# Attention feeding a two-expert mixture on one Trainium2 core: the front of the kernel reordered across GpSimd, VectorE, ScalarE and the queues

## The chip, the cores and the metric

The kernel runs on one core of a Trainium2 chip. A core has a matrix engine, TensorE (PE in the profile, with PEld for its weight loads), VectorE (DVE), ScalarE (ACT), GpSimd (POOL) and SyncE (SP), which here only issues transfers. Each engine works through its own list of instructions in order, and instructions of different engines meet at semaphores. 16 DMA engines move data between HBM and the on-chip memory.

The metric is the device time of one execution in microseconds. Three runs of the kernel before took 718.5, 725.89 and 728.75 us; their median, 725.89 us, is the number to compare with. One further execution was profiled.

## The reference

A causal linear attention with a decay per head is followed by a mixture of eight experts, of which each token uses two.

```python
def _attn_ref(q, k, v):                       # 4 batches, 8 heads, 768 tokens, 64 wide
    for t in range(S):
        state = gamma * state + outer(k[:, :, t], v[:, :, t])
        y[:, :, t] = scale * (q[:, :, t] @ state)

def _moe_ref(x, w_gate, w_noise, noise, w1, w2):   # x: 3072 tokens x 512
    noisy = x @ w_gate + log1p(exp(x @ w_noise)) * noise
    top2 = np.argpartition(-noisy, 2, axis=1)[:, :2]
    top2_w = softmax over the two
    for e in range(8):                         # w1[e]: 512 x 1024, w2[e]: 1024 x 512
        h = np.maximum(x[mask] @ w1[e], 0.0)
        out[mask] += top2_w * (h @ w2[e])
```

## The kernel before

The work has three stages on the same core.

**The chunk loop** (the loop over `j` in `range(NCH)`, 24 iterations) computes attention for 128 tokens at a time. Six chunks make a batch (`NC = 6`). Iteration `j` issues, in this order: the scores of the next chunk on PE (`qk(j+1)`, L311); on GpSimd the scaled values of the next chunk and the scaled queries of the one after (`v_scale`, tile `vp`, L285; `q_scale`, tile `qs`, L291); loads of chunk `j+4` on the SP queue; on VectorE the masked scores (`masked(j+1)`, tile `am`, L318) and the low half of the last output (`x_lo`, L352); the work listed in `between[j]`; then on PE the output of chunk `j` (`y_mm`, L325, L329, and the state update `pU`, L334) and the router's logits of chunk `j-3` (L364, L367); last the work listed in `todo[j]`. ScalarE copies the state (`U`, L340), sums squares (`junk`, L343) and writes the high half `x` (L348). The first chunk of a batch has no L329, the last no L334. The scores' PSUM has three buffers and a chunk uses two, so `qk(j+1)` waits for the first mask of chunk `j`.

**Routing.** For each batch `b`, steps `route_a` to `route_g` run on VectorE some iterations later, as `todo` places them. `route_e(b, k)` builds one-hot tables `ob` (L492) and `a` (L494) and multiplies three of five value planes into `bb` (L501); `route_e2(b, k)` does the other two planes on GpSimd (L501 too). `table(b)` is twelve matmuls over `a` and `bb` (L511), `route_f` adds their result to `acc`, `slots` turns it into row numbers `idx`, and `gather` fetches 128 rows of `xbuf` by an indirect transfer that GpSimd issues (tile `xg`, L621). `x_t` transposes them into `xe` through the SP queue. `places(b)` (L423) needs the choice of experts, `mb`, from `route_b2`.

**Expert weights.** A matrix comes in four parts. Each is loaded into `wst` (`w_load`, SP), its squares are summed on ScalarE (`w_sum`, L180), and then one scale for the four is made through a tiny matmul on PE (`w_scale`, L184). `w_hi` (L197, ScalarE) writes the high half. The low half comes in one of two ways:

```python
    def w_lo(e, which, i):
        nc.vector.scalar_tensor_tensor(lo, st[:, i * 1024:(i + 1) * 1024], sc[:, 0:1], hi,
                                       op0=OP.mult, op1=OP.subtract)

    def w_lo_pool(e, which, i):
        nc.scalar.activation(s, s, AF.Copy, scale=sc[:, 0:1])
        nc.gpsimd.tensor_tensor(lo, s, hi, op=OP.subtract)
```

The first is one VectorE instruction (L202); the second is one of ScalarE (L209) and one of GpSimd (L210).

**The early units.** After the loop, expert 0 starts on tokens that are already routed while the last batch is still being routed. Twenty `units` hold PE work: eight first products over 384 columns (`mm1`, L715 to L717, each followed by `hh` on ScalarE, L718, and `hl` on VectorE, L719), three second products (`mm2`, L745 to L747), eight first products over 192 columns, one more `mm2`. `early(n)` issues the next `n`; between the calls stand the routing steps. The first unit reads the 384 columns of `xe` that the first three gathers fill. `pH`, the PSUM of `mm1`, has three buffers, each freed by `hl`. `ranks()` orders the experts by load (L541 to L560, all on VectorE); the loads of the next expert need its result.

**The experts** then run one after the other, each with its next expert's weights prepared beside it.

Of the kernel before, what the change touches and what calls it, by code (L numbers as in the profile page):

```python
# [19 lines left out]
B, H, S, D = 4, 8, 768, 64  # L20
C = 128
NC = S // C
NCH = B * NC
# [11 lines left out]
B0 = B // 2  # L35
# [3 lines left out]
NBLK, CAP = 7, 832  # L39
CAPS = [832, 832, 816, 800, 800, 784, 768, 768]  # L40
NCOL = NBLK * E
# [53 lines left out]
def moe_kernel(ctx, tc, qT, kT, kt, vt, noise, wgn, w1, w2, ctab, qtab, xbuf, out):  # L95
# [434 lines left out]
    def rows_of(tk, n0, n1):  # L530

        padv = work.tile([128, NCOL], F32, name="padv")
        nc.vector.tensor_scalar(padv[:, n0:n1], tk[:, n0:n1], 0.0, K("pad"), op0=OP.is_equal, op1=OP.mult)
        nc.vector.scalar_tensor_tensor(idx[:, n0:n1], tk[:, n0:n1], 127.0, padv[:, n0:n1], op0=OP.add, op1=OP.add)

    def ranks():

        m = E - 1
        n, s3, s4 = R["cum"][:, 1:E], [128, m, m], [128, m, NBLK, m]
        key = hp.tile([128, m], F32, name="key")  # L540
        nc.vector.scalar_tensor_tensor(key, n, 8.0, K("tie"), op0=OP.mult, op1=OP.add)  # L541
        cm = hp.tile(s3, F32, name="cm")
        nc.vector.tensor_tensor(cm, key[:, None, :].to_broadcast(s3), key[:, :, None].to_broadcast(s3), op=OP.is_gt)
        rk = hp.tile([128, m], F32, name="rk")
        nc.vector.tensor_reduce(rk, cm, axis=AX.X, op=OP.add)
        pm = hp.tile(s3, F32, name="pm")
        nc.vector.tensor_tensor(pm, rk[:, None, :].to_broadcast(s3),
                                K("i64")[:, :m, None].to_broadcast(s3), op=OP.is_equal)
        nc.vector.tensor_tensor(cm, pm, K("lidx")[:, None, 1:E].to_broadcast(s3), op=OP.mult)
        nc.vector.tensor_reduce(rk, cm, axis=AX.X, op=OP.add)  # L550
        nc.vector.tensor_copy(eid, rk)
        tp = wp = hp.tile(s4, F32, name="tp")
        for t, a, d in ((tp, tk, tk), (wp, wacc, wacc)):
            v = a[:, NBLK:].rearrange("p (e t) -> p t e", e=m)
            nc.vector.tensor_tensor(t, v[:, None].to_broadcast(s4), pm[:, :, None, :].to_broadcast(s4), op=OP.mult)
            nc.vector.tensor_reduce(d[:, NBLK:].rearrange("p (r t) -> p r t", r=m), t, axis=AX.X, op=OP.add)
        rows_of(tk, NBLK, NCOL)
        nc.vector.tensor_tensor(cm, pm, K("rcap")[:, :, None].to_broadcast(s3), op=OP.mult)
        nc.vector.memset(capd, float(CAP))
        nc.vector.tensor_reduce(capd[:, 1:E], cm.rearrange("p r e -> p e r"), axis=AX.X, op=OP.add)  # L560
# [43 lines left out]
    def at(j, f, *a):  # L604
        todo.setdefault(j, []).append((f, a))
# [25 lines left out]
    between = {}  # L631
    for b in range(B - 1):
        n = (b + 1) * NC
        steps = [(2, route_a, b), (3, route_b, b), (4, route_b2, b), (4, route_c, b), (5, route_h, b), (5, route_d, b),
                 (6, route_e, b, 0), (6, route_e2, b, 0), (7, route_e, b, 1), (7, route_e2, b, 1), (8, route_f, b),
                 (8 if b == 0 else NCH - 1 - n, route_g, b)]
        if b == B - 2:
            steps = [(2, route_a, b), (3, route_b, b), (3, route_b2, b), (4, route_c, b), (4, route_h, b), (5, route_d, b)]
        else:
            between.setdefault(n + 8, []).append((table, b))  # L640
        between.setdefault(n + 5, []).append((places, b))
        for s in steps:
            at(n + s[0], *s[1:])
    at(0, gate_sum)
    at(1, gate_weights)
    for i in range(4):
        at(6 + 3 * i, w_load, 0, "1", i)
        at((8, 11, 14, 16)[i], w_sum, 0, "1", i)
        at((17, 18, 18, 19)[i], w_hi, 0, "1", i)
        at(19 + i, w_lo_pool, 0, "1", i)  # L650
        at(18 + i, w_load, 0, "2", i)
        at(19 + i, w_sum, 0, "2", i)
    at(2, nc.vector.tensor_copy, lanes, K("lanes"))
    at(2, nc.vector.tensor_copy, blks, K("blks"))
    between.setdefault(17, []).append((w_scale, 0, "1"))
    between[NCH - 1] += [(w_scale, 0, "2"), (w_hi, 0, "2", 0), (w_hi, 0, "2", 1)]
    at(NC * (B0 + 1) + 2, slots, 0, 3)
    for t in range(3):
        at(NC * (B0 + 1) + 2, gather, 0, t, 0, 128, B0 * S)
        at(NC * (B0 + 1) + 3, x_t, 0, t)  # L660
    mid = SECOND // 128
    at(1, nc.sync.dma_start, xbuf[:128, :], zero.bitcast(F16))

# [115 lines left out]
    def early(n):  # L779
        for _ in range(n):  # L780
            if units:
                units.pop(0)()

    early(1)
    logits(NCH - 3)
    w_hi(0, "2", 2)
    w_lo_pool(0, "2", 0)
    route_e(b - 1, 0)
    products(b - 1, 0, nc.vector, 3, NV)
    early(1)  # L790
    logits(NCH - 2)
    w_hi(0, "2", 3)
    w_lo_pool(0, "2", 1)
    early(2)
    logits(NCH - 1)
    route_a(b)
    w_lo_pool(0, "2", 2)
    early(1)
    w_lo_pool(0, "2", 3)
    route_b(b)  # L800
    route_b2(b)
    early(1)
    route_e(b - 1, 1)
    products(b - 1, 1, nc.vector, 3, NV)
    early(1)
    places(b)
    early(1)
    out_scale(0, 0, 3)
    early(1)
    table(b - 1)  # L810
# [18 lines left out]
        gather(0, t, SECOND - t * 128 if t == mid else 0)  # L829
    for t in range(mid, NBLK):  # L830
        x_t(0, t)
    slots(NBLK, NCOL)
    ranks()
    early(len(units))
    out_scale(0, mid, NBLK)
    for t in range(mid):
# [171 lines left out]
```

## Time and profile before

| what | us |
|---|---|
| median of three runs (lowest, highest) | 725.89 (718.5, 728.75) |
| profiled execution | 717.18 |
| its span, first to last instruction | 715.3 |
| PE busy in the span | 670.7 |
| first early unit starts on PE | 151.94 |
| last early unit ends, expert 0 goes on | 215.67 |

The span is 1.9 us short of the execution's own time. The profiled execution is faster than each of the three timed runs. In the views below times are in microseconds from the span's start, "idle before" is the time that an engine stood still before an instruction, with what ended it behind the arrow, and PEclk is the share of full clock speed that TensorE was granted.

### The profile page before, as it was taken

To read this page: it belongs to the slowest core of one execution; us is meant where nothing else is said; L and a number is where in the kernel's file an instruction comes from. 1 tells how busy PE (TensorE), PEld (TensorE's weight loads), DVE (VectorE), ACT (ScalarE), POOL (GpSimd) and SP (SyncE) were. 2 spreads that over 40 slices of the span, in tenths; PEclk is the share of its full clock that TensorE was granted. 3 is DMA by queue.
4 is the path that set the end of the run, shared out by engine and by line. 5 is a ranking of instruction groups with operands and counts; after the bars stand their busy time and mean duration, and the time that the engine had idled before them with its cause. 6 is when DMAs were issued, how large, how long until landed. Compare 5 with 4: busy or idle time off the path is not lost.

```text
span 715.3 us, 11986 instructions
## 1 busy us (share of the span) xinstructions
PE 670.7 (94%) x4789; PEld 420.0 (59%) x4789; DVE 292.6 (41%) x727; ACT 302.1 (42%) x544; POOL 232.7 (33%) x174
## 2 busy tenths in 40 slices
PE   8999888687979999999999999999999999999991
PEld 6999787663567654465455545554654465456540
DVE  4457978358642452624215321522152144215100
ACT  4544346372114744445344434444354454344110
POOL 3544736523343501440242043204312330340021
PEclk9999999678989999999999999999999999999996
DMA  9999999848169881668366546726681784371132
GB/s 332 323 322 326 351 317 279 202 109 317 45 143 295 145 272 31 119 110 262 48 131 160 175 89 120 219 87 118 120 271 30 132 192 150 73 133 30 16 44 31
DMA packets 116136, 119.22 MB, mean 167 GB/s; under 512 B 82608, under 2 KB 82864, under 8 KB 112496
## 3 DMA queue, kind: packets, MB, share of 16 engines
q1 hardware_dynamic: 104112, 91.25, 44.7%
q0 software_dynamic: 11392, 26.35, 19.9%
q8 instruction: 38, 0.62, 0.4%
q10 hardware_dynamic: 576, 0.85, 0.3%
q14 instruction: 18, 0.15, 0.1%
HBM read 72.80 MB, written 26.21 MB: 138 GB/s over the span
## 4 chain that ended last, share of the span: by engine, by line
PE 82%; DVE 6%; DMA 4%; POOL 2%; issue 2%; ACT 1%; SPq 1%; POOLq 0%; ACTq 0%
PE pH L715 12%; PE pH L716 12%; PE pH L717 12%; PE pO L745 11%; PE pO L747 11%; PE pO L746 11%; PE pY L325 4%; PE pA L311 2%; PE pY L329 2%; PE pU L334 2%; DVE bb L501 1%; DMA xbuf<-x 1%; DVE am L318 1%; DMA in_v<-vt 1%; DMA in_k<-kT 1%
## 5 line engine op out<-in xcount | busy, mean ns | idle before, releaser
L736 POOL DMA_INDIRECT out<-ot,idx x54 | 87.1, 1613 | 346.8 <-ACT ot L731 209.3
L715 PE MATMUL pH<-xe,w1h 128*128 128x384 f16 (+4 forms) x544 | 178.1, 327 | 4.7 <-DVE hl L719 4.7
L716 PE MATMUL pH<-xe,w1h 128*128 128x384 f16 (+4 forms) x544 | 178.2, 328 | 0.0
L717 PE MATMUL pH<-xe,w1l 128*128 128x384 f16 (+4 forms) x544 | 178.1, 327 | 0.0
L719 DVE SCALAR_TENSOR_TENSOR hl<-pH,hh 128x384 f16<-128x384 f32 (+4 forms) x136 | 74.4, 550 | 208.4 <-ACT hh L718 208.4
L745 PE MATMUL pO<-w2h,hh 128*128 128x512 f16 x384 | 145.9, 380 | 0.0
L747 PE MATMUL pO<-w2h,hl 128*128 128x512 f16 x384 | 145.8, 380 | 0.0
L746 PE MATMUL pO<-w2l,hh 128*128 128x512 f16 x384 | 145.8, 380 | 0.0
L718 ACT ACTIVATE hh<-pH 128x384 f16<-128x384 f32 (+4 forms) x136 | 65.7, 483 | 133.8 <-PE pH L717 133.8
L731 ACT ACTIVATE ot<-pO,gse 128x512 f32<-128x512 f32 (+4 forms) x54 | 37.1, 686 | 175.3 <-PE pO L747 170.8
L716 PEld LDWEIGHTS <-w1h 128*128 128x128 f16 x544 | 54.1, 99 | 38.0 <-issue 5.8
L202 DVE SCALAR_TENSOR_TENSOR w1l<-wst,wsc,w1h 128x1024 f16<-128x1024 f32 x28 | 35.7, 1283 | 99.0 <-ACT w1h L197 99.0
L717 PEld LDWEIGHTS <-w1l 128*128 128x128 f16 x544 | 54.2, 100 | 34.7 <-issue 1.0
L715 PEld LDWEIGHTS <-w1h 128*128 128x128 f16 x544 | 54.7, 101 | 33.2 <-issue 0.8
L621 POOL DMA_INDIRECT xg<-xbuf,idx x55 | 58.8, 1070 | 41.6 <-DVE wacc L527 20.7
L180 ACT ACTIVATE junk<-wst 128x1024 bf16<-128x1024 f32 x64 | 67.0, 1047 | 4.1 <-DMA wst<-w 4.0
L747 PEld LDWEIGHTS <-hl 128*128 128x128 f16 x384 | 37.6, 98 | 45.6 <-issue 0.5
L745 PEld LDWEIGHTS <-hh 128*128 128x128 f16 x384 | 38.3, 100 | 44.2 <-ACT hh L718 0.3
L746 PEld LDWEIGHTS <-hh 128*128 128x128 f16 x384 | 37.7, 98 | 44.4 <-issue 0.4
L325 PE MATMUL pY<-vp,am 128*128 128x64 f32 x384 | 50.7, 288 | 0.2
L325 PEld LDWEIGHTS pY<-vp,am 128*128 128x128 f32 x384 | 47.7, 202 | 2.8 <-DVE x L352 0.6
L285 POOL TENSOR_TENSOR vp<-in_v,ct 128x512 f32<-128x512 f32 x24 | 28.0, 1168 | 46.4 <-PE pU L334 17.3
(163 smaller groups left out, 725.6 us busy)
## 6 DMA issues: line engine op xcount, KB each, us to landing
wst<-w SPq DMA_DIRECT2D x28, 1024.0 KB, 7.5
in_q<-qT SPq DMA_DIRECT2D x24, 256.0 KB, 5.3
in_k<-kT SPq DMA_DIRECT2D x24, 256.0 KB, 5.4
in_v<-vt SPq DMA_DIRECT2D x24, 256.0 KB, 5.0
in_kt<-kt SPq DMA_DIRECT2D x24, 256.0 KB, 5.2
xbuf<-x SPq DMA_DIRECT2D x24, 256.0 KB, 4.8
out<-zero SPq DMA_DIRECT2D x6, 1024.0 KB, 9.6
wst<-w SPq DMA_DIRECT2D x8, 512.0 KB, 6.0
```

The costliest lines, as they stand in the source:

```text
L180: nc.scalar.activation(junk, st[:, i * 1024:(i + 1) * 1024], AF.Square, accum_out=ss[:, i:i + 1])
L325: nc.tensor.matmul(pY[:, 2 * i + s, :], AM[j][:, s, i, :], VP[j][:, 2 * i + s, :], start=(i == 0 and s == 0), stop=True, skip_group_check= ...
L621: nc.gpsimd.indirect_dma_start(out=x[:p1], out_offset=None, in_=xbuf[:128 + rows], in_offset=bass.IndirectOffsetOnAxis(ap=idx[:p1, i:i + 1 ...
L715: nc.tensor.matmul(p[:, :n], whi, xh, start=(k == 0), stop=False)
L716: nc.tensor.matmul(p[:, :n], whi, xl, start=False, stop=False)
L717: nc.tensor.matmul(p[:, :n], wlo, xh, start=False, stop=(k == KT - 1))
L718: nc.scalar.activation(hh[:, f, n0:n1], p[:, :n], AF.Relu)
L719: nc.vector.scalar_tensor_tensor(hl[:, f, n0:n1], p[:, :n], 0.0, hh[:, f, n0:n1], op0=OP.max, op1=OP.subtract)
L736: nc.gpsimd.indirect_dma_start(out=out, out_offset=bass.IndirectOffsetOnAxis(ap=idx[:n, i:i + 1], axis=0), in_=ot[:n], in_offset=None, com ...
L745: nc.tensor.matmul(p, a, WT["2h"][:, f, :], start=(f == 0), stop=False)
L746: nc.tensor.matmul(p, a, WT["2l"][:, f, :], start=False, stop=False)
L747: nc.tensor.matmul(p, c, WT["2h"][:, f, :], start=False, stop=(f == FT - 1))
```

## The change

It moves work between engines and to other iterations; what is computed stays the same.

```diff
+        yield
...
+        slots(NBLK, NCOL)
         for t, a, d in ((tp, tk, tk), (wp, wacc, wacc)):
...
+            yield
...
-                 (6, route_e, b, 0), (6, route_e2, b, 0), (7, route_e, b, 1), (7, route_e2, b, 1), (8, route_f, b),
+                 (6, route_e, b, 0), (7, route_e2, b, 0), (7, route_e, b, 1), (8, route_e2, b, 1), (9, route_f, b),
...
-            between.setdefault(n + 8, []).append((table, b))
+            between.setdefault(n + 9, []).append((table, b))
...
-        at(6 + 3 * i, w_load, 0, "1", i)
-        at((8, 11, 14, 16)[i], w_sum, 0, "1", i)
-        at((17, 18, 18, 19)[i], w_hi, 0, "1", i)
-        at(19 + i, w_lo_pool, 0, "1", i)
-        at(18 + i, w_load, 0, "2", i)
-        at(19 + i, w_sum, 0, "2", i)
+        at((4, 7, 10, 12)[i], w_load, 0, "1", i)
+        at((6, 9, 12, 14)[i], w_sum, 0, "1", i)
+        at((15, 16, 17, 18)[i], w_hi, 0, "1", i)
+        at((18, 19, 20, 20)[i], w_lo, 0, "1", i)
+        at((14, 16, 17, 18)[i], w_load, 0, "2", i)
+        at((16, 18, 19, 20)[i], w_sum, 0, "2", i)
+        at(21 + i // 2, w_hi, 0, "2", i)
...
-    between.setdefault(17, []).append((w_scale, 0, "1"))
-    between[NCH - 1] += [(w_scale, 0, "2"), (w_hi, 0, "2", 0), (w_hi, 0, "2", 1)]
-    at(NC * (B0 + 1) + 2, slots, 0, 3)
+    between.setdefault(15, []).append((w_scale, 0, "1"))
+    between.setdefault(21, []).append((w_scale, 0, "2"))
+    at(22, w_lo_pool, 0, "2", 0)
+    between[NCH - 1].append((w_lo_pool, 0, "2", 1))
+    at(NC * (B0 + 1) + 3, slots, 0, 3)
     for t in range(3):
-        at(NC * (B0 + 1) + 2, gather, 0, t, 0, 128, B0 * S)
-        at(NC * (B0 + 1) + 3, x_t, 0, t)
+        at(NC * (B0 + 1) + 3 + t // 2, gather, 0, t, 0, 128, B0 * S)
+        if t < 2:
+            at(NC * (B0 + 1) + 4, x_t, 0, t)
+    between[NCH - 1].append((x_t, 0, 2))
...
+    w_lo_pool(0, "2", 2)
+    w_lo_pool(0, "2", 3)
     early(1)
     logits(NCH - 3)
-    w_hi(0, "2", 2)
-    w_lo_pool(0, "2", 0)
...
-    early(1)
+    early(2)
     places(b)
-    early(1)
     out_scale(0, 0, 3)
...
-    slots(NBLK, NCOL)
-    ranks()
+    early(1)
+    for piece in ranks():
+        early(2)
```

The other steps of `w_hi` and `w_lo_pool` that stood among the early units are removed there in the same way. Behind the early units the lists of all engines are the same.

On GpSimd, in the last four iterations of the loop and behind it, stood before (`vp`, `qs`: values and queries of a chunk; `w1l`, `w2l`: low parts of expert 0's weights; `xg`: a gather):

```order
L501 TENSOR_TENSOR bb<-ob,vv 128x6x112
L210 TENSOR_TENSOR w1l<-wst_622,w1h 128x1024
L285 TENSOR_TENSOR vp<-in_v,ct 128x512
L291 TENSOR_TENSOR qs<-in_q,gq 128x512
L210 TENSOR_TENSOR w1l<-wst_622,w1h 128x1024
L621 DMA xg<-xbuf,idx 128x1024 x3
L285 TENSOR_TENSOR vp<-in_v,ct 128x512
L291 TENSOR_TENSOR qs<-in_q,gq 128x512
L210 TENSOR_TENSOR w1l<-wst_622,w1h 128x1024
L285 TENSOR_TENSOR vp<-in_v,ct 128x512
L210 TENSOR_TENSOR w1l<-wst_622,w1h 128x1024
L210 TENSOR_TENSOR w2l<-wst_1570,w2h 128x1024 x4
```

Now, on the same engine from the same table part on:

```order
L501 TENSOR_TENSOR bb<-ob,vv 128x6x112
L285 TENSOR_TENSOR vp<-in_v,ct 128x512
L291 TENSOR_TENSOR qs<-in_q,gq 128x512
L624 DMA xg<-xbuf,idx 128x1024 x2
L285 TENSOR_TENSOR vp<-in_v,ct 128x512
L210 TENSOR_TENSOR w2l<-wst_1229,w2h 128x1024
L624 DMA xg<-xbuf,idx 128x1024
L210 TENSOR_TENSOR w2l<-wst_1229,w2h 128x1024 x3
```

The four `w1l` are gone from GpSimd, the last `qs` stands ahead of the gathers, and the third gather stands behind the first `w2l`.

On VectorE, iterations 18 and 19 of the loop (`p2m`, `upx`: the scale of an output chunk) read before:

```order
L352 SCALAR_TENSOR_TENSOR x_1526<-pY,upx,x_1526 128x512
L492 TENSOR_TENSOR ob<-blks,lf 128x336
L494 TENSOR_TENSOR a<-lanes,lf 128x768
L501 TENSOR_TENSOR bb<-ob,vv 128x6x168
L156 TENSOR_SCALAR p2m<-xss 128x1
L157 TENSOR_SCALAR upx<-p2m 128x1
L318 TENSOR_TENSOR am<-pA,ct 128x512 x2
```

And now, at the same place:

```order
L352 SCALAR_TENSOR_TENSOR x_1535<-pY,upx,x_1535 128x512
L492 TENSOR_TENSOR ob<-blks,lf 128x336
L494 TENSOR_TENSOR a<-lanes,lf 128x768
L501 TENSOR_TENSOR bb<-ob,vv 128x6x168
L202 SCALAR_TENSOR_TENSOR w1l<-wst_506,wsc_508,w1h 128x1024
L156 TENSOR_SCALAR p2m<-xss 128x1
L157 TENSOR_SCALAR upx<-p2m 128x1
L318 TENSOR_TENSOR am<-pA,ct 128x512 x2
```

One `w1l` has come between a table part and the next masks; iteration 19 has the same, iteration 20 has two.

On ScalarE, iterations 22 and 23 and the first units stood before (`U`: state copies; `junk`: sums of squares; `hh`: a unit's result):

```order
L340 ACTIVATE U_162<-pU 64x4x64 x2
L343 ACTIVATE junk,xss<-pY 128x512
L209 ACTIVATE wst_622<-wst_622,wsc_624 128x1024
L180 ACTIVATE junk,wss_1571<-wst_1570 128x1024
L348 ACTIVATE x_1904<-pY,upx 128x512
L197 ACTIVATE w2h<-wst_1570,wsc_1572 128x1024 x2
L343 ACTIVATE junk,xss<-pY 128x512
L348 ACTIVATE x_1980<-pY,upx 128x512
L718 ACTIVATE hh<-pH 128x384
L197 ACTIVATE w2h<-wst_1570,wsc_1572 128x1024
L209 ACTIVATE wst_1570<-wst_1570,wsc_1572 128x1024
L718 ACTIVATE hh<-pH 128x384
```

And now:

```order
L340 ACTIVATE U_162<-pU 64x4x64 x2
L343 ACTIVATE junk,xss<-pY 128x512
L197 ACTIVATE w2h<-wst_1229,wsc_1231 128x1024 x2
L209 ACTIVATE wst_1229<-wst_1229,wsc_1231 128x1024
L348 ACTIVATE x_1912<-pY,upx 128x512
L209 ACTIVATE wst_1229<-wst_1229,wsc_1231 128x1024
L343 ACTIVATE junk,xss<-pY 128x512
L348 ACTIVATE x_1982<-pY,upx 128x512
L209 ACTIVATE wst_1229<-wst_1229,wsc_1231 128x1024 x2
L726 ACTIVATE hh<-pH 128x384 x4
```

The first L209 of `w2`, on which the first `w2l` of GpSimd waits, now stands behind two `w2h` of iteration 22, and no weight work is left between the units.

More of the change, by code (lines that the diff above doesn't have):

```diff
@@ L791, in moe_kernel @@
     logits(NCH - 2)
-    w_hi(0, "2", 3)
-    w_lo_pool(0, "2", 1)
     early(2)
@@ L796, in moe_kernel @@
     route_a(b)
-    w_lo_pool(0, "2", 2)
     early(1)
-    w_lo_pool(0, "2", 3)
     route_b(b)
```

## The prediction

> **What bounds the kernel now.** The page comes first: TensorE is busy 94% of the span, and nearly all of its slices under 90% lie in the first 12 of 40.
>
> ```profile
> PE 670.7 (94%) x4789; PEld 420.0 (59%) x4789; DVE 292.6 (41%) x727; ACT 302.1 (42%) x544; POOL 232.7 (33%) x174
> PE   8999888687979999999999999999999999999991
> ```
>
> The table by stretches splits this: the second half of the chunk loop, the early units, the experts. The columns are the stretch, its length, then the busy time of PE, PEld, DVE, ACT and POOL, granted clock, DMA share, GB/s.
>
> ```profile
> 66.00:152.00 86.00, 67.87 (x677) 64.10 (x675) 62.48 (x216) 42.16 (x87) 46.21 (x32) 0.89 0.95 264
> 152.00:216.00 64.00, 55.01 (x351) 33.79 (x348) 41.34 (x121) 16.48 (x32) 22.94 (x14) 0.88 0.59 173
> 216.00:715.00 499.00, 484.05 (x3123) 264.36 (x3120) 154.07 (x281) 211.47 (x345) 133.09 (x98) 0.99 0.56 128
> ```
>
> From 216 on TensorE is full, and the change touches nothing there, so that part only shifts. What can move is the 18 us without PE work in the loop and the 9 us among the units, besides the clock. The table of waits names them (total, times, longest), the first three rows for 66 to 152, the last two for 152 to 216:
>
> ```profile
> PE pA L311 <- POOL qs L291: 9.4, 3, 6.2
> PE pR L184 <- ACT junk L180: 5.1, 2, 3.2
> PE pR L511 <- DVE p2m L156: 3.0, 2, 1.5
> ...
> PE pH L715 <- DVE hl L719: 4.7, 2, 4.3
> PE pR L423 <- DVE mb L413: 4.3, 1, 4.3
> ```
>
> **The loop with its waits gone.** One undisturbed iteration stands in the chain of waits: scores, output, state, update, next scores, 5.05 us in all. Beside it stand the timeline's rows of the last scores of the loop (iteration 22), the first unit, and the first product behind the units.
>
> ```profile
> 86.42 1.09 PE pA L311 x16
> 87.51 1.93 PE pY L325 x16
> 89.44 0.95 PE pY L329 x8
> 90.39 0.89 PE pU L334 x8
> 91.47 1.09 PE pA L311 x16
> ...
> 133.62 2.08 PE L311 MATMUL pA<-qs,in_k 64*128 64x128 f32 x16 [6.15 <-POOL qs L291]
> 151.94 0.48 PE L715 MATMUL pH<-xe,w1h 128*128 128x384 f16 x1
> 215.67 0.27 PE L715 MATMUL pH<-xe,w1h 128*128 128x256 f16 x1
> ```
>
> The change aims at each wait ahead of 133.6: all 9.4 on `qs` (GpSimd's `bb`, `w1l` and gathers no longer stand ahead of it), the 3.0 of the table (an iteration later), and of the two scale waits the first, 5.1 - 3.2 = 1.9. Without them iteration 22 would start at 133.6 - 14.3 = 119.3. Half clock before 152 goes with the gap of 6.2. Four things come back.
>
> (a) `masked` still comes behind VectorE's table parts of iterations 12 and 13: an estimate of 0.5 us, what is left of the table's wait once PE meets the masks instead.
>
> (b) The scale of `w1` now stands in iteration 15. It waits for the fourth `w_sum`, which stands in ScalarE's list behind the Exp and Ln of `route_a`, and these wait for VectorE to come through the second table part, masks, `x_lo`, `route_g` and `route_a`. From 81.7, where the table part ended, that is by estimate 4.6 us of VectorE, 0.5 of Exp and Ln and 1.2 of `w_sum`: 88.0, while PE is there at 84.5. The 3.5 shrink where GpSimd no longer slows the table part. I take 2.4; ends 0.5 and 3.5.
>
> (c) VectorE in iterations 18 to 21. By form, and from the page:
>
> ```profile
> L318 DVE TENSOR_TENSOR am<-pA,ct 128x512 f32<-128x512 f32 x23 | 14.8, 681 | 5.4 <-PE pA L311 5.4
> L352 DVE SCALAR_TENSOR_TENSOR x<-pY,upx,x 128x512 f16<-128x512 f32 x13 | 9.7, 744 | 5.5 <-ACT x L348 5.5
> L501 DVE TENSOR_TENSOR bb<-ob,vv 128x1008 bf16<-128x1008 bf16 x4 | 9.3, 2320 | 0.0
> L494 DVE TENSOR_TENSOR a<-lanes,lf 128x768 bf16<-128x768 bf16 x4 | 3.8, 951 | 0.0
> L492 DVE TENSOR_TENSOR ob<-blks,lf 128x336 bf16<-128x336 bf16 x4 | 2.0, 498 | 0.0
> L202 DVE SCALAR_TENSOR_TENSOR w1l<-wst,wsc,w1h 128x1024 f16<-128x1024 f32 x28 | 35.7, 1283 | 99.0 <-ACT w1h L197 99.0
> ```
>
> A plain iteration costs it two `am`, one `x` and 0.3 for the scale: 2.4. Iterations 18 and 19 add 0.5 + 0.95 + 2.32 and one `w1l` of 1.28: 7.45 each. Iteration 20 has two `w1l` and `route_a` (1.0): 6.0. Iteration 21 has `route_b`, `route_b2`, `route_f`, the `w2` scale and `slots`, some 4.6: 7.0. Together 27.9, against PE's 4.15 (first chunk of a batch) + 5.05 + 5.05 + 6.2 (with table and scale) = 20.4. VectorE enters with a lead of about 5.05 - 2.4 = 2.6, so PE waits 27.9 - 20.4 - 2.6 = 4.9. The ends come from two more rows, VectorE's two products of a later table part while GpSimd stood still, and GpSimd's own `bb`:
>
> ```profile
> 174.52 1.97 DVE L501 TENSOR_TENSOR bb<-ob,vv 128x1008 bf16<-128x1008 bf16 x2
> ...
> L501 POOL TENSOR_TENSOR bb<-ob,vv 128x672 bf16<-128x672 bf16 x4 | 7.9, 1964 | 8.7 <-DMA in_q<-qT 4.6 <-DVE ob L492 4.1
> ```
>
> The first holds five planes, so three took 3/5 of 1.97, 1.2 instead of 2.32; that takes 2.2 off the two: 2.7. Each of the four `w1l` held for a whole `bb` of GpSimd (second rival), 1.97, gives 12.8. I take 4.9, nearest to the forms' means, since GpSimd's part is in each of them already.
>
> (d) The scale of `w2` in iteration 21 needs the load issued in iteration 18, two iterations earlier. Ends: 0, and 3.2 as before; I take 1.8.
>
> Iteration 22 then starts at 119.3 + 0.5 + 2.4 + 4.9 + 1.8 = 128.9, 4.7 sooner than before.
>
> **From there to the first unit.** The third gather, which the first unit needs, now stands on GpSimd behind the first `w2l`, and that behind ScalarE's L209 and two L197 of iteration 22, which stand behind the update of that iteration. Rows: ScalarE and GpSimd in 66 to 152 by form, then issue to landing at 185 to 204, when the queues were quiet (median us).
>
> ```profile
> L340 ACT ACTIVATE U<-pU 64x256 f32<-64x256 f32 x20 | 7.5, 376 | 19.9 <-PE pU L334 19.7
> L209 ACT ACTIVATE wst<-wst,wsc 128x1024 f32<-128x1024 f32 x4 | 4.5, 1135 | 0.0
> L197 ACT ACTIVATE w2h<-wst,wsc 128x1024 f16<-128x1024 f32 x2 | 2.2, 1140 | 1.3 <-DVE wsc L157 1.3
> L210 POOL TENSOR_TENSOR w1l<-wst,w1h 128x1024 f16<-128x1024 f32 x4 | 9.5, 2370 | 12.1 <-ACT wst L209 12.1
> ...
> xg<-xbuf,idx POOLq DMA_INDIRECT x5, 3.3
> xe<-xg SPq DMA_TRANSPOSE x5, 3.3
> ```
>
> PE to the end of its update 4.9; two U and one `junk` 1.6; two L197 2.3; L209 1.1; L210 2.1 to 2.4; gather 3.3; transpose 3.3, on an SP queue that waits for it with the last `x_out` and the zeroing of `out` behind: 18.9, and 0.5 of handovers: the first unit can start at 128.9 + 19.4 = 148.3. PE's own loop ends about 8.2 after the start of iteration 22, at 137.1, so it stands idle 11.2 us where before it went on at once. This is where most of the loop's gain is lost: the first unit comes 3.6 us sooner, not 15.
>
> **The units.** Before they took 215.7 - 151.9 = 63.7. Out of that go the waits 4.7 + 4.3 = 9.0: `places` now has two units ahead of it and no weight part on GpSimd or ScalarE in `route_b`'s way, and `ranks` lets two units' `hl` pass between its pieces. Out goes also half clock: 64 x 0.12 = 7.7 by the table, 6.5 of it while PE worked. That leaves 48.2. Back come 3.4 for the clock behind the idle 11.2 (next part) and 1.6 for `ranks`, whose 5.6 us on VectorE still compete with `hl`. So 53.2, ending at 201.5. The loads of expert 1 wait for `ranks`' first piece, which ends sooner; they cost nothing as long as PE has the rest of expert 0's products over them.
>
> **The clock.** The 4.3 us wait before `places` brought half speed for some 7 us; the 1.9 us wait at 98 brought none:
>
> ```profile
> 95.00:100.00 5.00, 3.07 (x45) 2.82 (x44) 2.54 (x15) 2.94 (x8) 2.27 (x2) 1.00 1.08 357
> 170.00:175.00 5.00, 2.92 (x16) 1.56 (x16) 4.25 (x27) 0.97 (x3) 0.00 (x0) 0.59 1.04 387
> 175.00:180.00 5.00, 5.00 (x20) 2.08 (x19) 4.17 (x17) 0.49 (x1) 0.00 (x0) 0.72 0.16 60
> ```
>
> So the idle 11.2 costs half of 6.8, 3.4 us. The waits (b) and (c) lie between the two cases; I count half of one such stretch, 1.7, ends 0 and 3.4. [...]
>
> **Sum.** The end of the units is 201.5 + 1.7 = 203.2 against 215.7, a gain of 12.5. On the profiled execution's 717.18 that is 704.7. The timed runs of before lie 1.3 to 11.6 above the profiled one, 8.7 in the median; nothing in the trace says why. I carry 7 of it: 712 us. The ends: with (a) 0.5, (b) 0.5, (c) 2.7, (d) 0 and no extra clock the gain is 20.1, 697.1, and with the lowest run's 1.3, 698; with (b) 3.5, (c) 12.8, (d) 3.2 and 3.4 of clock hardly 0.4 is left, and between that and the forecast, at a gain of 1.5 and the median's 8.7, stands 724.
>
> **Rivals.** First, VectorE keeps up: GpSimd's `bb` an iteration later leaves it alone, and (b) and (c) are at their low ends. For it speaks that `bb` is slow only beside GpSimd's work. Time 712 - 1.9 - 2.2 - 1.7 - 1.8 = 704.
>
> Second, `w1l` on VectorE is held by GpSimd. At 166 to 170 two small VectorE operations with two on-chip inputs lasted 1.4 and 2.1 us, for 48 elements each, until one and the other of GpSimd's two `w2l` ended:
>
> ```profile
> 165.74 4.21 POOL L210 TENSOR_TENSOR w2l<-wst,w2h 128x1024 f16<-128x1024 f32 x2 [2.50 <-ACT wst L209]
> 166.55 1.39 DVE L394 TENSOR_TENSOR sp<-sp,nz 128x48 f32<-128x48 f32 x1
> 167.97 2.05 DVE L396 TENSOR_TENSOR ny<-sp,lg 128x48 f32<-128x48 f32 x1
> ```
>
> `w1l` has two such inputs, and iterations 19 and 20 hold a `bb`, a `vp` and a `qs` of GpSimd. Each held for a `bb`: 4 x 1.97 = 7.9 more, time 720. [...]
>
> Third, slower: the eight weight loads now fall into iterations 4 to 18, where the DMA share is 0.95. If each `w_sum` of `w2` (16, 18, 19, 20) waits for its part with the high half of `x` behind it in ScalarE's list, VectorE and then PE wait too. From 3.1 us beyond cover for each the gain is gone; at 4.5 the loop is 18 longer: 730. Against it: loads land 6.1 us after issue, two iterations are 10, and the longest such wait before was 2.3:
>
> ```profile
> wst<-w SPq DMA_DIRECT2D x7, 512.0 KB, 6.1
> ACT junk L180 <- DMA wst<-w: 4.0, 3, 2.3
> ```
>
> Fourth, the loop wins nothing, because late queries take the place of late `qs`; iteration 22 stays at 133.6, the units still gain: 712 + 4.7 = 717.
>
> **Chances.** Forecast 0.53 (its own range 706 to 718), VectorE keeps up 0.15, `w1l` held 0.20, loop wins nothing 0.07, slower 0.05. The range 698 to 724 leaves out about 0.15. A measurement of this kernel tells about 2% from no change, here 711.4 and 740.4: faster by more than that are half of the forecast's cases and nearly all of the first rival's, 0.42; slower 0.02; within it 0.56.
>
> **What would show it.** A PE wait of about 11 us on `xe` ahead of L715 after the last loop matmul, with half clock behind it; if it is under 5, the chain through `w2l` is wrong. PE waits on `qs` at zero; on `am` some 5 us in iterations 18 to 21; on L184 two of about 2. `w1l` on VectorE at 1.3 each, or at 2 and more by the second rival. No wait before `places`, none over 1 in the 192-column products. It is wrong if ScalarE waits on `wst` for more than 5 us, or if the experts' stretch gets longer.

## The result and the profile after

Twenty runs of each kernel were compared in the end. The changed kernel takes 717.28 us in the median (712.71 to 722.55), the kernel before 721.88 (718.3 to 728.75); the ratio is 0.9934, with an interval of 0.9906 to 0.9962. So the change is a gain of 0.7%, where 1.9% had been forecast (712 against 725.89). The profiled execution of the changed kernel took 716.62 us with a span of 714.2, beside 717.18 and 715.3 before.

The table of waits of TensorE over the whole span of the changed kernel (total, times, longest) shows that the waits on `qs`, the table, `mb` and the weight scales are gone, all but 1.8 us (the 1.4 on `qs` lie ahead of 60 us). Others stand there:

```profile
PE pH L723 <- DMA xe<-xg: 12.8, 2, 8.5
PE pA L311 <- DVE am L318: 3.8, 3, 2.2
PE pH L723 <- DVE hl L727: 2.2, 1, 2.2
PE pY L325 <- DVE dn L433: 2.0, 1, 2.0
...
PE pA L311 <- POOL qs L291: 1.4, 1, 1.4
...
PE pR L184 <- ACT junk L180: 0.4, 2, 0.2
```

The table by stretches of the changed kernel, cut as before (stretch, length, PE, PEld, DVE, ACT, POOL, clock, DMA share, GB/s):

```profile
66.00:152.00 86.00, 71.10 (x676) 66.60 (x672) 72.79 (x223) 44.05 (x89) 39.88 (x31) 0.83 0.92 259
152.00:216.00 64.00, 61.81 (x449) 40.49 (x448) 37.74 (x126) 16.70 (x40) 17.04 (x13) 0.98 0.70 217
216.00:714.00 498.00, 476.54 (x3017) 255.78 (x3014) 150.64 (x273) 204.35 (x328) 129.38 (x98) 0.98 0.55 122
```

The units have become dense: 61.8 of 64 us at a clock of 0.98, where it was 55.0 at 0.88. The loop has lost clock, 0.83 for 0.89. And in the experts' stretch, which had no wait of TensorE to speak of behind 216 and a clock of 0.99, TensorE now stands still for 21.5 of 498 us, where it was 15 of 499, the span's tail; the clock is 0.98.

Where the gain stays can be followed along a few points of TensorE's list. The rows of the changed kernel's timeline: last scores of the loop, first unit, last table, first product behind the units, first product of expert 1; then the rows of the kernel before for the last table and for expert 1.

```profile
131.24 1.16 PE L311 MATMUL pA<-qs,in_k 64*128 64x128 f32 x16
150.86 0.48 PE L723 MATMUL pH<-xe,w1h 128*128 128x384 f16 x1 [8.54 <-DMA xe<-xg]
185.90 1.59 PE L511 MATMUL pR<-bb,a 128*128 128x280 bf16 x12
202.78 0.27 PE L723 MATMUL pH<-xe,w1h 128*128 128x256 f16 x1
230.97 0.50 PE L723 MATMUL pH<-xe,w1h 128*128 128x416 f16 x1 [4.25 <-DMA xe<-xg]
```

```profile
193.91 1.59 PE L511 MATMUL pR<-bb,a 128*128 128x280 bf16 x12
239.44 0.34 PE L715 MATMUL pH<-xe,w1h 128*128 128x416 f16 x1
```

| point | before | after | sooner by |
|---|---|---|---|
| iteration 22's scores | 133.62 | 131.24 | 2.4 |
| first unit | 151.94 | 150.86 | 1.1 |
| last table (`table(b)` of the last batch; the expectations below call it the third) | 193.91 | 185.90 | 8.0 |
| units end | 215.67 | 202.78 | 12.9 |
| expert 1 begins | 239.44 | 230.97 | 8.5 |
| span | 715.3 | 714.2 | 1.1 |

Up to the end of the units the whole gain is there: 12.9, forecast 12.5. Then 4.4 go in a new wait of 4.25 on expert 1's tokens, and 7.4 more behind it. Of these, half clock took 2.7 (the 5.7 us from 230.9 on ran at 0.53), short stops between 360 and 510, for which the profile shows no releaser, took 2.3, and a drop of the clock at 430 to 450 some 1.7. The last two go with the chip more than with the change: such stops, 0.3 to 3.0 us in all behind 60, stand in the profiles of all ten experiments below from e5 on, two with the old loop among them, and in none of e1 to e4, which were measured together on one chip. The drop is one stretch of 3.4 us at half clock (437.6 to 441.05), at the last of three of the stops (to 436.14, 437.22 and 437.99); e6_w2_later, e10_table_old and e12_best have drops of that size too, between 500 and 600 (a clock of 0.91 over 20 us, twice in the first, once in each of the others). That the chip makes them is a reading: which chip the two profiles compared here were taken on is not on record.

Why the tokens came late stands in GpSimd's timeline of the changed kernel (L744 is a scatter of a finished block into `out`, L624 a gather):

```profile
192.86 1.62 POOL L744 DMA_INDIRECT out<-ot,idx  x1 [0.30 <-issue]
198.61 1.57 POOL L744 DMA_INDIRECT out<-ot,idx  x1 [4.13 <-ACT hh L726]
204.21 1.56 POOL L744 DMA_INDIRECT out<-ot,idx  x1 [4.03 <-ACT ot L739]
215.72 1.56 POOL L744 DMA_INDIRECT out<-ot,idx  x1 [9.94 <-DMA out<-ot,idx]
217.59 1.02 POOL L624 DMA_INDIRECT xg<-xbuf,idx  x1 [0.30 <-issue]
```

Each scatter adds into `out` and waits until the one ahead of it has landed (the fourth for 9.94 us here); where a row names another engine, that one came at about the same time. The second was followed after 5.6 us, the third only after 11.5: on SP, the four loads of expert 1's weights, 4 MB, had been issued from 203.17 on. Expert 1's gathers stand behind the fourth scatter. Before, the same events ran as in the rows below: the third and fourth scatter and the first gather of expert 1, then, from the view of the tile `xe`, the fourth transposition with its time from issue to landing.

```profile
212.03 1.56 POOL L736 DMA_INDIRECT out<-ot,idx  x1 [3.85 <-DMA out<-ot,idx]
222.19 1.56 POOL L736 DMA_INDIRECT out<-ot,idx  x1 [8.59 <-ACT hh L718]
224.06 1.02 POOL L621 DMA_INDIRECT xg<-xbuf,idx  x1 [0.30 <-issue]
...
L628 SPq DMA_TRANSPOSE xe<-xg x1: 1287/1287/1287, 233.7 to 233.7; - x1
...
DMA to landing us min/median/max: 3.2/3.2/3.2
```

So the fourth transposition landed at 236.85, 2.6 us ahead of TensorE. From the last table to expert 1 it is 45.5 us before and 45.1 after; the chain itself, from the last table to that landing, took 42.9 before and about 45 after, when TensorE waited for its end. The change shortened TensorE's own work over that stretch, but not this chain. It became the path.

### The profile page after: what moved, and what is told of

It reads as the page before. It is cut to its first block, busy times and chain, and to the rows that moved or that the text cites. A ratio compares the mean times of both kernels' runs of the same rounds, so it can differ in the third digit from the quotient of the medians.

```text
span 714.2 us, 11981 instructions
## 1 busy us (share of the span) xinstructions
PE 672.1 (94%) x4789; PEld 420.2 (59%) x4789; DVE 296.2 (41%) x731; ACT 298.2 (42%) x540; POOL 216.2 (30%) x170
## 4 chain that ended last, share of the span: by engine, by line
PE 82%; DMA 6%; DVE 5%; issue 2%; ACT 2%; POOL 1%; SPq 1%; POOLq 0%; ACTq 0%
PE pH L725 12%; PE pH L723 12%; PE pH L724 12%; PE pO L753 11%; PE pO L755 11%; PE pO L754 11%; PE pY L325 4%; PE pA L311 2%; DMA out<-ot,idx 2%; PE pY L329 2%; PE pU L334 2%; DMA xg<-xbuf,idx 1%; DMA xe<-xg 1%; DVE am L318 1%; DMA in_v<-vt 1%
## 5 line engine op out<-in xcount | busy, mean ns | idle before, releaser
L744 POOL DMA_INDIRECT out<-ot,idx x54 | 85.8, 1589 | 357.7 <-ACT ot L739 232.2
L202 DVE SCALAR_TENSOR_TENSOR w1l<-wst,wsc,w1h 128x1024 f16<-128x1024 f32 x32 | 41.7, 1313 | 99.0 <-ACT w1h L197 99.0
L624 POOL DMA_INDIRECT xg<-xbuf,idx x55 | 56.7, 1030 | 55.7 <-DVE wacc L527 23.4
L285 POOL TENSOR_TENSOR vp<-in_v,ct 128x512 f32<-128x512 f32 x24 | 25.9, 1080 | 61.5 <-issue 24.5
```

The lines of the kernel that those rows point to most:

```text
L624: nc.gpsimd.indirect_dma_start(out=x[:p1], out_offset=None, in_=xbuf[:128 + rows], in_offset=bass.IndirectOffsetOnAxis(ap=idx[:p1, i:i + 1 ...
L744: nc.gpsimd.indirect_dma_start(out=out, out_offset=bass.IndirectOffsetOnAxis(ap=idx[:n, i:i + 1], axis=0), in_=ot[:n], in_offset=None, com ...
```

## The experiments

Theory A: that chain (last table, last gathers of expert 0, scatters one behind the other, one of them beside 4 MB of loads, gathers and transpositions of expert 1) took the gain. The rivals were: something in the experts themselves (B), `ranks` in pieces making expert 1 late (C), GpSimd's order alone without the loads (D). Each ratio is to the kernel before on the same chip, with its interval; the changed kernel stands at 0.9934. Three chips were used, one for e1 to e4, one for e5 to e12, one for e13 and e14, and the changed kernel itself was not run again beside them.

**e1_gathers.** The changed kernel, with expert 1's gathers taken out from behind the scatters:

```diff
     for t in range(mid):
         put(0, t, first[t])
+        if t == 0:
+            for u in range(4):
+                gather(1, u)
...
-            ahead = [lambda t=t: (gather(e + 1, t), x_t(e + 1, t)) for t in blocks(e + 1)]
+            ahead = [lambda t=t: (e == 0 and t < 4 or gather(e + 1, t), x_t(e + 1, t)) for t in blocks(e + 1)]
```

> The changed kernel with the four gathers of expert 1 issued right behind the first scatter of expert 0, ahead of the other three. Theory A (the units' gain of 12.9 us is lost again because expert 1's tokens come late: the third scatter, 204.21, lands only after some 11 us beside the 4 MB of weight loads issued at 203.17, the fourth scatter waits for it, and the gathers stand behind that one on GpSimd): PE's wait of 4.2 us on xe goes, and with it the half clock behind it, 3.4 us; about 7.6 us faster than the changed kernel, near 710 us, ratio to before near 0.983. Theory B (the loss lies in the experts themselves, by instruction issue and clock, and the wait on xe is incidental): the wait goes and the time does not move by more than 2 us, ratio 0.991 to 0.994. Theory C (ranks in pieces sends expert 1's loads off too late, and its weights are the next thing late): the wait turns into one on the weights of expert 1 of about the same length, ratio 0.993.

Measured: 706.5 us against 718.58, ratio 0.9833 (0.9774 to 0.9893). As Theory A had it, 0.983. The gathers now run at 197.35 to 203.5, and expert 1 starts without a wait, 38.6 us behind the last table. Its timeline row, and the one wait that came behind it, on the last block of expert 1:

```profile
225.75 0.34 PE L723 MATMUL pH<-xe,w1h 128*128 128x416 f16 x1
...
245.61 0.34 PE L723 MATMUL pH<-xe,w1h 128*128 128x416 f16 x1 [2.25 <-DMA xe<-xg]
```

**e4_before_gathers.** The same two edits in the kernel before, where by Theory A nothing waits for those gathers.

> The kernel before with the same move of expert 1's four gathers. Theory A: there the fourth block of xe landed at 236.85 and PE came to it at 238.9, so nothing waited for it: no change, ratio 0.997 to 1.003. If the loads that stand beside the scatters cost PE something in another way (by clock or by shared transfers), it gains half a per cent or more here too.

Measured: 0.9992 (0.995 to 1.0034): nothing, as expected. By these ratios the cure is worth about 1% in the changed kernel and nothing in the one before. Two pairs below that differ by the cure alone, each on one chip, give somewhat less: 4.2 us from e2_third to e3_both and 4.5 us from e7_before_units to e9_units_gathers, about 0.6%, with intervals that overlap. B falls as the main cause: the wait was not incidental. e4_before_gathers leaves the loads where they were, so it does not say whether they cost something in another way.

**e5_ranks_whole.**

```diff
-    for piece in ranks():
-        early(2)
+    list(ranks())
```

> The changed kernel with ranks in one piece again, at the place where its first piece stands. Theory A (expert 1's tokens hang on the third table, the last gathers of expert 0, the scatters and the loads beside them; ranks is not in that chain): the second-layer wait of some 4.3 us on hl and half clock for 3.4 us come back among the 192-column units, which end near 208 instead of 202.8, while expert 1 still starts near 231, with a shorter wait on xe; time within 3 us of the changed kernel, ratio 0.990 to 0.995. Theory C (the pieces make expert 1's loads and tokens late): expert 1 starts 4 to 6 us sooner, ratio near 0.986.

Measured: 0.9978 (0.9939 to 1.0018), some 3 us slower than the changed kernel, a little beyond what A allowed. The units ended at 206.4 with one wait of 3.8 on `hl`, and expert 1 started at 233.35, later and not sooner; there it waited 2.2 us, by the profile for ScalarE's squares and not for its tokens. C falls: `ranks` in pieces does not make expert 1 late. That it is a gain, 3.6 us at the end of the units, is not clear of noise in the times. The loads didn't move with `ranks`: the number of the next expert that they need is there at 190.8, and on SP they come 5.5 us behind the last transposition of expert 0 in both kernels (205.2 to 210.69 before, 197.7 to 203.17 after).

**e6_w2_later** and **e13_loads_last** take the loads away from beside the scatter: the first puts the two of `w2` behind expert 1's transpositions, the second all four (and expert 1's squares of `w1` behind the next second product).

```diff
-    for w in "12":
-        w_load(1, w, 0, 2)
-        w_load(1, w, 2, 2)
+    w_load(1, "1", 0, 2)
+    w_load(1, "1", 2, 2)
...
-        if more and e:
+        if more:
             w_load(e + 1, "2", 0, 2)
             w_load(e + 1, "2", 2, 2)
+        if more and e:
             w_scale(e + 1, "1")
```

> The changed kernel with the two loads of w2 of expert 1 (2 of the 4 MB) issued on SP behind the first four transpositions of expert 1 instead of ahead of them; the gathers stay where they were on GpSimd. Theory A: with half the bytes beside it the third scatter lands in about half of its 11.5 us, the fourth scatter and the gathers follow some 5.5 us sooner, the wait of 4.2 us on xe and the half clock behind it go: about 7 us faster than the changed kernel, ratio 0.982 to 0.985. Theory D (the order on GpSimd alone makes the gathers late, whatever the loads do, or w2 then comes too late for its squares): no more than 2 us faster, ratio 0.990 to 0.994.

Measured: 0.9931 (0.9895 to 0.9966), no better than the changed kernel, in the range of D. The profiled execution, the slowest of its twelve, is no clean case of D: nothing waited on expert 1's tokens there, since TensorE came to them only at 235.41, 44.2 us behind the last table. With 2 MB beside it the third scatter still held the next one for 9.5 us (209.64 to 219.10), although the loads were through at 217 (the DMA share fell from 1.02 to 0.20 there): half the bytes saved 2 us, not 5.5. And a wait of 2.7 us on the squares of `w2` had come, at 245.

> The changed kernel with all four loads of expert 1 (4 MB) issued behind its first four transpositions, and the squares of its w1 behind the next second product; the scatters and gathers stay where they were on GpSimd. It measures what the loads do to the scatters, not a better kernel: w1 will be late. Theory A (the loads stretch the third scatter from about 4.8 to some 11 us): the third scatter lands in 4.5 to 5.5 us, the fourth scatter is issued 5 to 7 us sooner, and from the third table to the landing of expert 1's fourth transposition it takes 38 to 40 us instead of 45; PE then waits 4 to 10 us on the squares of w1; time 0.990 to 1.003. Theory D (the scatter is slow whatever stands beside it): the third scatter takes 9 to 11 us and the 45 us stay.

Measured: 1.0135 (1.0102 to 1.0168), slower, by a wait of 17.5 us on the squares of `w1`, more than expected. What was to be measured, the scatters, came out as A had it:

```profile
204.78 1.56 POOL L744 DMA_INDIRECT out<-ot,idx  x1 [3.86 <-ACT hh L726]
210.24 1.56 POOL L744 DMA_INDIRECT out<-ot,idx  x1 [3.89 <-ACT hh L726]
212.11 1.02 POOL L624 DMA_INDIRECT xg<-xbuf,idx  x1 [0.31 <-issue]
```

Without loads the scatter holds the next for 5.5 us, and the first gather of expert 1 stands 25.3 us behind the last table (186.79 there) instead of 31.7; the fourth transposition is issued 34.6 us behind it instead of 41.0. So the loads make 6 of the 45 us; the rest is order: four scatters in a row, then the gathers. 2 MB slowed the scatter nearly as much as 4: it held the next for 9.5 and 11.5 us, for 5.5 with none. Why half the bytes did not halve the loss is not shown.

**e2_third** and **e3_both** try the other loss, the 8.5 us ahead of the first unit.

```diff
-        at(NC * (B0 + 1) + 3 + t // 2, gather, 0, t, 0, 128, B0 * S)
-        if t < 2:
-            at(NC * (B0 + 1) + 4, x_t, 0, t)
-    between[NCH - 1].append((x_t, 0, 2))
+        at(NC * (B0 + 1) + 3, gather, 0, t, 0, 128, B0 * S)
+        at(NC * (B0 + 1) + 4, x_t, 0, t)
```

> The changed kernel with the third gather of expert 0 issued in iteration 21 with the other two, ahead of the first w2l on GpSimd, and its transposition with theirs. Theory A (PE's 8.5 us ahead of the first unit are the chain ScalarE L209, GpSimd w2l, third gather, transposition, and the last batch's routing follows PE): the first unit starts 6 to 8 us sooner, the units end 6 to 8 sooner and expert 1's tokens come sooner by as much, with the wait on them still there at about 4 us; 6 to 8 us faster than the changed kernel, 709 to 711 us, ratio about 0.984. Theory B (behind the units a fixed chain from the last batch's routing decides): the units start sooner, but PE then waits for mb before places or longer on xe of expert 1, and no more than 2 us are left; ratio 0.991 to 0.993.

Measured: 0.987 (0.9818 to 0.9923). The first unit came 17.5 us behind iteration 22's scores instead of 19.6, so the edit is worth 2.1 there and not 6 to 8. The third gather was issued at 137.71, 6.2 sooner, but took 7.1 us to land with two transpositions beside it, and VectorE was later with the last chunk (a wait of 3.3 on `g`). Behind the units TensorE then waited 7.3 on expert 1's tokens instead of 4.25: expert 1 began at 230.05, only 0.9 sooner. That is Theory B of this experiment in the trace. The ratio looks better than that, but its interval overlaps with the changed kernel's, so nothing is built on it.

> Both edits, of e1_gathers and e2_third. Theory A: they add, 7.6 and 6 to 8 us, 702 to 704 us, ratio 0.972 to 0.976. If either is bounded by the routing of the last batch, the sum stops at the larger of the two, ratio 0.983.

Measured: 0.9816 (0.9751 to 0.9882), no further than e1_gathers within the intervals. They don't add within what the times can tell.

**e8_gathers_w2** puts e1_gathers and e6_w2_later together.

> Both cures in the changed kernel: expert 1's first four gathers behind the first scatter (e1_gathers) and its w2 loads behind the first four transpositions (e6_w2_later). Theory A: either cure alone takes the wait ahead of expert 1 away, so they do not add; what e1_gathers still had, a wait of 2.3 us on xe at 245.6 (the last blocks of expert 1, whose gathers stand behind scatters), may shrink: ratio 0.980 to 0.984. If the loads cost the experts more than through that wait, 0.975 or less.

Measured: 0.9881 (0.983 to 0.9931), not better than the gathers alone, a little outside what was expected. **e12_best** adds to e3_both that expert 1's last three gathers go ahead of expert 0's later scatters (`if e == 0 and ahead:` in place of `if e == 0 and n >= 4:`).

> e3_both (third gather with the other two; expert 1's first four gathers behind the first scatter) with expert 1's last three gathers also ahead of expert 0's later scatters, so that its second half doesn't wait. Theory A: the wait of 1.6 to 2.3 us on xe at 245 to 248 goes, nothing else: 1.5 to 2.5 us faster than e3_both, ratio 0.977 to 0.980. Rival (the scatters, each behind the other's landing, now end later and hold ot or the next expert's gathers): no change, 0.981 to 0.984, with a wait on ot or on xe of expert 2.

Measured: 0.9852 (0.9798 to 0.9905). The wait at 245 is gone, the time is not: the rival's outcome, though the waits that it named, on `ot` or on expert 2's tokens, do not stand in the profile. e1_gathers, with two edits, is the version to keep; it beats both kernels by these ratios, and no other was shown to beat it.

**Which part brings what.** With the cure in place the parts can be told apart. **e7_before_units** and **e9_units_gathers** are the kernel before with only the last part of the change, without and with the cure:

```diff
-    early(1)
+    early(2)
     places(b)
-    early(1)
...
-    slots(NBLK, NCOL)
-    ranks()
+    early(1)
+    for piece in ranks():
+        early(2)
```

> The kernel before with only the last part of the change: places behind two units, ranks in pieces between products. Iterations of the loop, weight steps and the early weight work stay as before. Theory A: the units lose the wait of 4.3 on mb, one of 4.3 on hl and half clock for some 6.8 us, and end 12 to 15 us sooner, 201 to 204 instead of 215.7; the third table comes 7.7 sooner, and 45 us behind it expert 1 starts, 231 instead of 238.9, with a wait of 4 to 6 on xe and half clock behind it: 3 to 5 us faster, ratio 0.993 to 0.996, as much as the whole change. If the chain behind the table did not decide, all of the units' gain would pass: ratio 0.980.

> e7_before_units with expert 1's four gathers behind the first scatter: the last part of the change alone, with the chain behind the third table shortened. Theory A (in e7 the units ended 5.5 us sooner than before, and PE then waited 3.8 us on xe and ran at part of its clock behind it): the wait and the half clock go, expert 1 starts 4 to 5 us sooner than in e7 and the time is 5 to 7 us under the kernel before: ratio 0.988 to 0.993. What is then left to the same cure on the whole change (0.983) is the loop's part, 4 to 6 us. If the loop's part of the change were worth nothing, this comes to 0.983.

Measured: 0.994 (0.9904 to 0.9975) without, 0.988 (0.9834 to 0.9926) with the cure. So this part alone gives what the whole change gave, though its units ended at 210.2 and not at 201 to 204, since a wait of 2.3 on `mb` and the weight steps were still there. **e14_front_gathers** is the other half: e1_gathers with this part undone.

> e1_gathers with the last part of the change undone: places behind one unit, ranks in one piece ahead of the remaining units. So the iterations of the loop, the weight work and the cure for expert 1 alone. With the other three of the four combinations (0.9992 with the cure alone, 0.988 with the units' part, 0.983 with both) the parts add if this comes to 0.992 to 0.996. Theory A: the loop's own gain is small (the same loop brought iteration 22 to between 131.2 and 136.7 in eight kernels, and the old one to 133.5 to 135.5 in four), and what the front part gives comes from the weight work that no longer stands between the units: 0.990 to 0.996. If the loop's waits were gone as the prediction has it: 0.983 to 0.988. If the front part gives nothing: 0.997 to 1.001.

Measured: 0.9904 (0.988 to 0.9928). The four combinations under the cure are 0.9992 (neither part), 0.988 (units), 0.9904 (loop and weights), 0.9833 (both). They stem from three chips, so differences of a few tenths of a per cent between them mean little.

**e10_table_old** and **e11_w1_pool** undo one piece of the loop's part in e1_gathers: the table's iterations (`(6, route_e2, b, 0)`, `(7, route_e2, b, 1)`, `(8, route_f, b)`, `table` at `n + 8`), and `w_lo` (back to `w_lo_pool`).

> e1_gathers (the changed kernel with the cure, ratio 0.983) with the table parts, the table and route_f of the first two batches back at their old iterations, GpSimd's products beside VectorE's. By the terms of the prediction: the table's wait of about 3.0 us on VectorE comes back less the 0.5 of its masks, and one or two waits on qs of 1 to 3 us, as GpSimd's product stands ahead of vp and qs: 2.5 to 6 us slower than e1_gathers, ratio 0.987 to 0.992. Rival (the wait for the masks and the locks of small VectorE operations, which fell into iterations 11 and 12 of the changed kernel, cost as much as the table's wait did): within 1.5 us, ratio 0.981 to 0.985.

> e1_gathers with the low parts of w1 back on ScalarE and GpSimd (L209, L210) at the iterations in which VectorE makes them in the changed kernel. By the terms of the prediction: VectorE is rid of four times 1.28 and PE's waits on masks and on dn in iterations 18 to 23 (about 3.5 us and half clock for some 7) go, but four times 2.37 stand ahead of vp and qs on GpSimd again and PE waits on qs for 3 to 6: between 1 us faster and 4 us slower than e1_gathers, ratio 0.982 to 0.989. Rival (VectorE was the bound of these iterations and GpSimd had room): 3 to 6 us faster, ratio 0.975 to 0.979.

Measured: 0.9958 (0.9923 to 0.9993) and 0.9888 (0.9854 to 0.9923). The table one iteration later is worth more than expected, about 1.2% by ratios from two chips: with it undone, 3.0 of waits on the table and 4.2 on `qs` came back. `w1` on VectorE is worth half a per cent by the medians, at the edge of the expected range, with intervals that overlap; that VectorE was the bound is out.

## Why the prediction was wrong, point by point

- **The step that failed** is "From 216 on TensorE is full, and the change touches nothing there, so that part only shifts", with "they cost nothing as long as PE has the rest of expert 0's products over them" on the loads of expert 1. I took an absence of waits for room. The profile of before had the number: the fourth transposition of expert 1 landed 2.6 us ahead of its use, at the end of a chain that began at the last table. A change that takes 12.9 us of TensorE's time out ahead of that point, and only 8.0 out ahead of the last table, gains 4.9 on the chain and must meet it. The 2.3 that are over the lead, and some 2.1 by which the chain itself took longer, are the new wait; the half clock behind it makes 7 us together. The prediction's own sign of being wrong, a longer stretch of the experts, came: 511.4 us from the end of the units to the end of the span, 499.6 before. Shown by e1_gathers and e4_before_gathers, on one chip: with the chain cut the change is worth 0.9833 to 0.9992, about 1.6% or 11 us, where the sum had 12.5.
- **The sum to the end of the units** came out at 202.8 for a forecast of 203.2, but by errors that cancel. The waits on `qs`, the table and the scales went as said; what came back ahead of iteration 22 was 11.9 (131.24 less the 119.3 without waits), where (a) to (d) made 9.6 and the clock 1.7. Inside it the parts were others: far more clock, less of (b), (c) and (d). The units made up for the rest.
- **(a)** was 0.5, for masks behind the table parts. Masks made TensorE wait 2.2, but ahead of the table parts, by small operations of the routing. **The clock** was 1.7, with 3.4 as its end; two stretches at half clock, of 10.2 and 6.8 us, took 8.5. The two belong together, as the last section shows. Nor did all of the half clock ahead of 152 go with the gap of 6.2 in the kernel before: there it ran from 130.0 to 143.7 and, behind the wait of 3.2 on the scale of `w2`, from 147.0 to 153.8.
- **(b)** and **(d)**, 2.4 and 1.8, measured 0.2 each. For (b) this is one case: seven of the nine other kernels with this loop wait 1.4 to 3.6 us there. That lateness ahead of the two scales had given ScalarE its time is likely and not shown. **(c)**, 4.9, measured 1.7 on masks; another 2.0 on `dn` came behind iteration 22. Of the four `w1l` of iterations 18 to 20 three took 1.27 and one, which met a `qs` of GpSimd, 2.29. So one was held, for 1.0 us, and not four for a whole `bb`, 7.9: the second rival is out at its price.
- **The loop's gain.** Iteration 22 was to come at 128.9 and came at 131.24. Ten kernels share this loop up to there, and their profiles have it between 131.2 and 136.7, 133.0 in the mean; in four with the old loop it stands between 133.5 and 135.5, 134.5 in the mean. So the loop's own gain is 1 to 2 us, nearer to the fourth rival than to the forecast. What the loop's part gives (e14_front_gathers) it gives mostly by taking weight work from between the units: the wait of 4.3 on `mb` is gone there.
- **The 19.4 us from iteration 22 to the first unit** measured 19.6, and 18.9 to 20.1 in six more kernels that gather in this order. The price was right, its main cause less so: e2_third took the `w2l` out of the chain and won 2.1 (1.9 in e3_both, 0.9 in e12_best).
- **The units**, 53.2, measured 51.9, with a wait of 2.2 on `hl` in the 192-column products, where none over 1 had been expected.
- **The offset.** Of the 8.7 us between the profiled run of before and its median I carried 7. With twenty runs that distance is 4.7, and in the changed kernel it is 0.7: the first three runs lay high and the profile low. This explains nothing of the miss, it hides part of it: in the profile's own terms 704.7 had been forecast and 716.62 measured, 11.9 apart, in the medians 712 and 717.28.
- **The rivals.** None of them had the mechanism. The time of the fourth, 717, was met by chance.

## What to carry to other kernels

Before a stretch is called unbounded because nothing waits there, take the latest arrival of each thing that it needs, and compare its lead with the time that is to be taken out ahead; a lead of 2.6 us does not cover the 4.9 that TensorE gained on the chain here. Look for the event from which that chain starts, and count as gain only what comes out ahead of it and what the lead covers. And where transfers each wait for the landing of the one before, put what the next stage needs ahead of them in the queue, and keep bulk loads from beside them where nothing needs those as soon (beside 4 MB a scatter held the next for 11.5 us, without for 5.5; but held back in e13_loads_last, the loads cost a wait of 17.5 us).

## What the runs showed of the hardware that was not expected

**Half clock with waits of 2.2 and 1.4 us.** The prediction had a wait of 1.9 us without half clock and one of 4.3 with it. In the changed kernel a wait of 2.17 us on masks (to 72.85) and one of 1.41 (to 115.89) both came with it: from 72.41 for 10.2 us, and from 116.78 for 6.8:

```profile
72.40:82.60 10.20, 9.75 (x58) 9.44 (x60) 9.91 (x14) 4.19 (x10) 3.65 (x3) 0.50 1.15 332
82.60:116.80 34.20, 32.22 (x357) 30.30 (x355) 27.05 (x96) 19.77 (x43) 19.28 (x16) 1.00 1.08 329
116.80:123.60 6.80, 6.80 (x34) 6.54 (x32) 6.77 (x10) 2.36 (x5) 2.29 (x2) 0.50 1.07 290
```

TensorE is busy in all of the first stretch but the end of its wait (9.75 of 10.20 us), and in the whole of the second (6.80 of 6.80). In the profiles of the kernel before and of the changed one, up to the tail of the span, each stretch at half clock lasts 3.41, 6.83, 10.24 or 13.65 us, 3.41 or a multiple of it. The length of a wait alone does not tell whether half clock comes: the one of 1.93 us before (97.88 to 99.81) stands in a stretch at full clock, 97.00 to 129.97, and is longer than the 1.41 that came with half clock here. What decides is not shown. Nor did it last alike with TensorE busy throughout: some 3.4 us in e7_before_units, from 174.3 to 177.7 behind a wait of 2.34 (one product of L748 took 0.63 us there, 0.38 ahead of it and behind), and 6.8 from 116.8 on here.

**VectorE's small operations beside GpSimd.** Three of them ahead of the masks, of 0.17 to 0.19 us each at their shortest, took 2.6 us more than that beside GpSimd's `vp` and `qs`, which makes them the likely cause of the wait of 2.17 us. From the timelines of VectorE and GpSimd of the changed kernel:

```profile
66.70 0.82 DVE L449 CAST vv<-g 128x12 bf16<-128x12 f32 x1
67.55 0.17 DVE L450 TENSOR_TENSOR gr<-g,vv 128x12 f32<-128x12 f32 x1
67.76 1.27 DVE L451 CAST vv<-gr 128x12 bf16<-128x12 f32 x1
...
70.62 1.04 DVE L478 TENSOR_SCALAR lb<-si 128x12 int32<-128x12 int32 x1
...
66.43 1.04 POOL L285 TENSOR_TENSOR vp<-in_v,ct 128x512 f32<-128x512 f32 x1 [2.42 <-DMA in_v<-vt]
67.73 1.26 POOL L291 TENSOR_TENSOR qs<-in_q,gq 128x512 f32<-128x512 f32 x1 [0.25 <-DMA in_q<-qT]
70.59 1.04 POOL L285 TENSOR_TENSOR vp<-in_v,ct 128x512 f32<-128x512 f32 x1 [1.60 <-DMA in_v<-vt]
```

Each of the two casts and L478 ends within 0.05 us of the GpSimd operation beside it. By their rows they read one tile each (`g`, `gr`, `si`), where the two operations in the rows of the second rival read two. Later in the same profile, from 104.54 on, the three took 0.73 (to 105.27; a `qs` of GpSimd ran to 105.22), 0.19 and 0.17 us, and at 66.92 to 70.18 in the kernel before 0.18, 0.18 and 0.17. Such differences may be a source of the 5 us by which the same loop scattered; that is an estimate and was not tried.
